# A fourth output buffer, an expert unit moved to another pair, and the last rows stored in two column halves

## The chip, the cores and the metric

The kernel runs on one core of one Trainium2 chip. The metric is the device time of one execution in microseconds, median of several runs. Before the change it is 336.73 us (three runs: 335.08, 336.73, 341.14). The profiled execution of it took 335.81 us, and its profile spans 334.1 us.

## The reference

Attention with a window and some global tokens over 8 batches of 8 heads, 576 tokens and 64 channels, then a feed-forward layer ("expert") with a squared ReLU over the 4608 tokens that come out:

```python
scores = scale * np.matmul(q, k.transpose(0, 1, 3, 2))        # per batch and head, 576 x 576
mask = np.abs(pos[:, None] - pos[None, :]) <= 32
mask = mask | is_global[:, None] | is_global[None, :]         # 8 global tokens
scores = np.where(mask, scores, -1e9)
attn = softmax(scores)
x = matmul(attn, v)  ->  (4608 tokens, 512)
h = x @ w_in                                                  # 512 -> 2048
r = np.maximum(h, 0.0)
out = (r * r) @ w_out                                         # 2048 -> 512, float32
```

## The kernel before

The attention of one batch is done in four pairs of heads. The expert layer works on chunks of 512 tokens, one chunk behind the attention, and is cut into units that are put between the steps of a pair, so that TensorE has work while ScalarE and VectorE (DVE) make the softmax. A chunk has 16 units of the first layer (`mm1`: four matmuls, a ReLU on ScalarE, a square on DVE) and 16 of the second (`mm2`: four row blocks of 128 tokens in four parts each; after the fourth part DVE copies the block from PSUM into an output buffer, and SyncE stores it).

```python
def expert_bank():                       # four PSUM banks in turn: three "mm", one "tr"
    banks["n"] += 1
    return pst("tr" if banks["n"] % 4 == 0 else "mm", [P, 512])

def mm1(c, u):
    ...
    for t in range(NDM):                 # 4
        nc.tensor.matmul(ph, w_in[:, t, u * P : (u + 1) * P], xT[:, t, ...], ...)   # L524
    rl = sbt("rl", [P, TC], FP16, bufs=3)
    nc.scalar.activation(out=rl, in_=ph, func=AF.Relu)                              # L529
    nc.vector.tensor_tensor(out=gts[c][:, u, :], in0=rl, in1=rl, op=ALU.mult)       # L530

def mm2(c, m, part):
    if part == 0:
        po_now[0] = expert_bank() if c else pst("mm", [P, 512])
    po = po_now[0]
    for f in range(part * 4, part * 4 + 4):
        nc.tensor.matmul(po, gts[c][:, f, m * P : (m + 1) * P], w_out[:, f, :], ...)  # L566
    if part == 3:
        ot = sbt("ot", [P, dm], FP32, bufs=3)
        nc.vector.tensor_copy(out=ot, in_=po)                                       # L572
        r0 = c * TC + m * P
        nc.sync.dma_start(out=out[r0 : r0 + P, :], in_=ot)                          # L574
```

One pair of heads, with `take(k)` issuing the next k units of the queue. `n` gives how many come before the outputs of the first half, between the two halves, and after the second half:

```python
def unit(i, n, nxt=None):
    scs = [scores(i, half, pair_tag[half], WIN2) for half in range(2)]     # matmuls, L621
    et = [weights(half, scs[half], WIN2) for half in range(2)]             # exp on ScalarE L630, mask on DVE L634
    take(n[0])
    ...
    for half in range(2):
        acc = outputs(i, half, et[half], pair_tag[half], WIN2, ...)        # matmuls, L663
        finish_outputs(i, half, acc, ...)     # ScalarE L686, L687: 1/sum; DVE L702 sums, L714 writes xT
        if half == 0:
            take(n[1])
    if i % NHP == NHP - 1:
        scatter(i // NHP)                     # DVE L733: the global tokens' rows into xT
    take(n[2])
```

The loop over the batches. In the first pair of a batch the copies of the next batch are put in: gathered and stored rows go through scratch memory, two transposing DMAs on SyncE bring the keys and queries, and five small copies on SyncE bring the values of the global tokens:

```python
for b in range(2, B):
    queue += units[b + 1]                     # one chunk: 32 units
    for hp in range(NHP):                     # 4 pairs
        unit(NHP * b + hp, ((2, 1, 4), (2, 1, 4), (2, 1, 5), (2, 1, 7))[hp])
        if hp == 0 and b + 1 < B:
            pool.tensor_copy(out=pin[0:1], in_=gsum[b][0:1, 0, 0, 0, 0:1])
            ...
            globals_to_scratch(b + 1)         # SyncE
            tokens_to_scratch(b + 1)          # GpSimd
            transposes(b + 1)                 # SyncE, L431
            vb[b + 1] = vb[(b + 1) % 2]
            values(b + 1)                     # GpSimd
            value_globals(b + 1)              # SyncE, L440
    take(99)
queue += units[B + 1] + units[B + 2]          # the last two chunks
take(999)
```

Of the kernel before, what the change touches and what calls it, by code (L numbers as in the profile page):

```python
# [8 lines left out]
FP32 = mybir.dt.float32  # L9
# [38 lines left out]
def kernel(  # L48
# [10 lines left out]
    nc = tc.nc  # L59
    B, H, S, D = q.shape  # L60
    NG = global_idx.shape[0]
    dm = H * D
    dff = moe_w_in.shape[1]
    P = 128
# [3 lines left out]
    NFF = dff // P  # L68
    NHP = H // 2
    TC = 512  # L70
    NCH = (B * S) // TC
# [6 lines left out]
    def sbt(name, shape, dtype, bufs=1, tag=None):  # L78
        return sb.tile(shape, dtype, name=name, tag=(tag or name), bufs=bufs)
# [5 lines left out]
    def pst(tag, shape, dtype=FP32):  # L85
        return ps.tile(shape, dtype, name=tag, tag=tag, bufs=bufs_of[tag])

    pool, dve, act = nc.gpsimd, nc.vector, nc.scalar
# [7 lines left out]
    w_out = sbt("w_out", [P, NFF, dm], FP16)  # L96
# [47 lines left out]
    for base, cu, cm in (  # L144
# [3 lines left out]
            out=ub[0], in_=ub[0], compare_op=ALU.is_ge, fill=0.0,  # L148
# [4 lines left out]
    for col, base, cm in ((slice(0, 2), -8, 1), (slice(1, 2), KN[-1] + 7, -1)):  # L153
        nc.gpsimd.affine_select(
            out=rows[:, col], in_=rows[:, col], compare_op=ALU.is_ge, fill=0.0,
# [3 lines left out]
        out=ub[1], in_=ub[0], compare_op=ALU.is_ge, fill=0.0,  # L159
# [9 lines left out]
        out=tok, in_=tok, compare_op=ALU.is_ge, fill=-1.0,  # L169
# [10 lines left out]
        out=identity, in_=identity, compare_op=ALU.not_equal, fill=1.0,  # L180
# [162 lines left out]
    def gather(c):  # L343
        for nm in "kqv":
            gst[(nm, c)] = sbt("gst" + nm, [P, D], FP16, bufs=2)
            pool.indirect_dma_start(
                out=gst[(nm, c)], out_offset=None,
                in_=src[nm].rearrange("b h s d -> (b h s) d"),
                in_offset=bass.IndirectOffsetOnAxis(ap=gidx[:, c : c + 1], axis=0),
            )  # L350
# [82 lines left out]
    def values(b):  # L433
        t = vb[b]
        for x in range(NT):
            fetch_values(b, x)
# [52 lines left out]
    def tr_k(i, op=None, tail=None, last=None, tag="mm"):  # L489
        op = op or dve.tensor_copy  # L490
        tk, gl = transposed("k", i, tag)
        kt = kts[i % NHP]
        op(
            out=kt[:, 0:4, 8:P].rearrange("p t (q j) -> p t q j", j=TJ),
            in_=tk[:, 0:80].rearrange("p (t q) j -> p t q j", t=4),
        )
        (tail or op)(
            out=kt[:, 4, 8 : 8 + KN[4]].rearrange("p (q j) -> p q j", j=TJ), in_=tk[:, 80:96]
        )
        (last or op)(out=kt[:, :, 0:NG], in_=gl.unsqueeze(1).to_broadcast((P, NT, NG)))  # L500

    def tr_q(i, op=None, tag="mm"):
        op = op or dve.tensor_copy
        tq, gl = transposed("q", i, tag)
        q4 = qts[i % NHP].rearrange("p (g x) -> p g x", x=GRP)
        op(
            out=q4[:, :, 0:GTOK].rearrange("p g (q j) -> p g q j", j=TJ),
            in_=tq.rearrange("p (g q) j -> p g q j", g=4),
        )
        op(out=q4[:, :, GTOK:GRP], in_=gl.unsqueeze(1).to_broadcast((P, 4, NG)))  # L510

    gts = {}
    banks = {"n": 0}

    def expert_bank():
        banks["n"] += 1
        return pst("tr" if banks["n"] % 4 == 0 else "mm", [P, 512])
# [40 lines left out]

    po_now = {}

    def mm2(c, m, part):
        if part == 0:
            po_now[0] = expert_bank() if c else pst("mm", [P, 512])
        po = po_now[0]
        for f in range(part * 4, part * 4 + 4):
            nc.tensor.matmul(  # L566
                po, gts[c][:, f, m * P : (m + 1) * P], w_out[:, f, :],
                start=(f == 0), stop=(f == NFF - 1),
            )
        if part == 3:  # L570
            ot = sbt("ot", [P, dm], FP32, bufs=3)
            nc.vector.tensor_copy(out=ot, in_=po)  # L572
            r0 = c * TC + m * P
            nc.sync.dma_start(out=out[r0 : r0 + P, :], in_=ot)  # L574

# [8 lines left out]
    queue = []  # L586

    def take(n):
        for _ in range(min(n, len(queue))):
            fn, a = queue.pop(0)  # L590
            fn(*a)
# [21 lines left out]
    def scores(i, half, tag, wins, sc=None):  # L613
        kt, qt = key_query(i)
        added = sc is not None
        if not added:
            sc = pst(tag, [P, 2, 512])
        for t, so, c0, w in wins[half]:
            for e in range(2):
                r = slice(64 * e, 64 * e + 64)  # L620
                nc.tensor.matmul(  # L621
                    sc[:, e, so : so + w], kt[r, t, :], qt[r, c0 : c0 + w],
                    start=not added, stop=True, skip_group_check=True,
                )
        return sc

    def weights(half, sc, wins, added=False):
        W = sum(x[3] for x in wins[half])
        et = sbt("et", [P, 2, SCW[0]], FP16, bufs=4)
        act.activation(  # L630
            out=et[:, :, 0:W], in_=sc[:, :, 0:W], func=AF.Exp, bias=0.0, scale=scale
        )
        if not added:
            dve.tensor_tensor(  # L634
                out=et[:, :, 0:W], in0=et[:, :, 0:W],
                in1=mask[:, MB[half] : MB[half] + W].unsqueeze(1).to_broadcast((P, 2, W)),
                op=ALU.mult,
            )
        return et
# [4 lines left out]
    def outputs(i, half, et, tag, wins, columns=False):  # L644
        b, hp = divmod(i, NHP)
        acc = pst(tag, [P, 2, 512])
        vt = vb[b]
        vtf = vt.rearrange("p t x d -> p t (x d)")
        nw = len(wins[half])
        for n, (t, so, c0, w) in enumerate(wins[half] if columns else ()):  # L650
            o = c0 - half * BANKC
            for x in range(2):
                for e in range(2):
                    nc.tensor.matmul(  # L654
                        acc[D * e : D * e + D, x, o : o + w],
                        one64 if x else vt[:, t, 4 * hp + 2 * e], et[:, e, so : so + w],
                        start=(n == 0), stop=(n == nw - 1), skip_group_check=True,
                    )
        for e in () if columns else range(2):
            for n, (t, so, c0, w) in enumerate(wins[half]):  # L660
                o = c0 - half * BANKC
                vo = D * (4 * hp + e)
                nc.tensor.matmul(  # L663
                    acc[:, e, o : o + w], vtf[:, t, vo : vo + P], et[:, e, so : so + w],
                    start=(n == 0), stop=(n == nw - 1), skip_group_check=True,
                )
        return acc
# [60 lines left out]
    def scatter(b, part=None, pairs=slice(0, NHP)):  # L728
        lo, hi = {
            None: (XOFF + b * S, XOFF + (b + 1) * S), 0: (0, HS + 1), 1: (XOFF + 255, XOFF + S),  # L730
        }[part]
        for g in range(NG):
            dve.tensor_copy(  # L733
                out=xT[:, pairs, lo:hi][:, :, ds(gvs[part][g], 1)],
                in_=gxs[b][:, pairs, g : g + 1],
            )
# [5 lines left out]
    def transposes0(hp):  # L742
# [11 lines left out]
        out=vb[0][0:NG, 0, 0 : 2 * H : 2], in_=idle[0:NG].rearrange("p (h d) -> p h d", d=D)  # L754
# [92 lines left out]
    def unit(i, n, nxt=None):  # L847
        scs = [scores(i, half, pair_tag[half], WIN2) for half in range(2)]
        et = [weights(half, scs[half], WIN2) for half in range(2)]
        take(n[0])  # L850
        if nxt:
            tr_k(nxt, tag="tr", tail=act.copy)
            tr_q(nxt, tag="mm", op=act.copy)
        for half in range(2):
            acc = outputs(i, half, et[half], pair_tag[half], WIN2, columns=i < 2 * NHP)
            finish_outputs(i, half, acc, columns=i < 2 * NHP)
# [3 lines that stand above are left out]
            scatter(i // NHP)  # L860
        take(n[2])
# [5 lines left out]
    for b in range(2, B):  # L867
        queue += units[b + 1]
        for hp in range(NHP):
            unit(NHP * b + hp, ((2, 1, 4), (2, 1, 4), (2, 1, 5), (2, 1, 7))[hp])  # L870
            if hp == 0 and b + 1 < B:
                pool.tensor_copy(out=pin[0:1], in_=gsum[b][0:1, 0, 0, 0, 0:1])  # L872
                if b == 2 or b % 2:
                    gather((b - 1) // 2)
                globals_to_scratch(b + 1)
                tokens_to_scratch(b + 1)
                transposes(b + 1)
                vb[b + 1] = vb[(b + 1) % 2]
                values(b + 1)
                value_globals(b + 1)  # L880
        take(99)
# [32 lines left out]
```

The softmax here doesn't subtract the row's maximum and nothing guards it: scores larger than these inputs give would overflow.

## Time and profile before

| what | value |
|---|---|
| device time, median of three runs | 336.73 us |
| profiled execution, span | 334.1 us |
| VectorE and ScalarE busy | 67% and 64% of the span |
| `L566` matmuls (second layer, "mm" banks) | 448, 103.9 us busy |
| `L524` matmuls (first layer, "mm" banks) | 384, 92.3 us busy |
| `L572` output copies | 36, 0.69 us each |
| stores of the output | 36, 256 KB each, on SyncE |

In what follows a line of a timeline has the start in us, the length, the engine, the line of the kernel, and the operation with its tiles; in brackets stand the idle time of the engine before it and what the profile names as its end. SPq lines are DMA issues on SyncE: their length is that of issuing, not of the transfer. Lines of stretches give for a window its length, then busy time (and number) of PE, PEld, DVE, ACT, POOL, then the granted TensorE clock, the busy share of the DMA engines and GB/s. A length of a matmul in the timeline is that of a pipelined instruction, so neighbours overlap.

### The profile page before, as it was taken

How to read it: one execution, taken by the hardware profiler on the slowest of the kernel's cores; microseconds unless marked ns; L12 is line 12 of the kernel's file. 1: busy time of each engine (PE TensorE's matmuls, PEld its weight loads, DVE VectorE, ACT ScalarE, POOL GpSimd, SP SyncE). 2: the span in 40 equal slices, each digit the busy share in tenths (PEclk: the TensorE clock that was granted, in tenths of full speed). 3: DMA queues.
4: the chain of work that ended last, by engine and by line, in shares of the span. 5: the costliest groups of instructions: out<-in, count | busy, mean ns of one | idle time of the engine just before them, and what ended most of it. 6: DMA issues, size and time to landing. Idle time of an engine off the chain costs nothing.

```text
span 334.1 us, 6749 instructions
## 1 busy us (share of the span) xinstructions
PE 317.7 (95%) x2377; PEld 163.6 (49%) x2377; DVE 224.1 (67%) x609; ACT 212.7 (64%) x425; POOL 106.7 (32%) x140
## 2 busy tenths in 40 slices
PE   7878899999999999899999999999999999999995
PEld 2557764444444544354545454445454554444442
DVE  7867955777768776687587866876878684323411
ACT  5777666669953995389539953896399626404600
POOL 8732477009900791078005930590000000000000
PEclk9999999999999999999999999999999999999999
DMA  7999999948996499899951999899710001011011
GB/s 203 189 204 207 203 160 139 172 138 61 143 143 169 32 139 134 178 100 134 121 169 33 123 140 175 114 130 141 128 63 3 31 33 63 0 65 63 1 65 63
DMA packets 148732, 38.20 MB, mean 114 GB/s; under 512 B 136802, under 2 KB 144090, under 8 KB 148698
## 3 DMA queue, kind: packets, MB, share of 16 engines
q0 software_dynamic: 104624, 17.37, 71.4%
q1 hardware_dynamic: 44072, 20.39, 31.6%
q8 instruction: 19, 0.31, 0.4%
q14 instruction: 15, 0.12, 0.1%
q10 hardware_dynamic: 2, 0.00, 0.0%
HBM read 37.36 MB, written 17.05 MB: 163 GB/s over the span
## 4 chain that ended last, share of the span: by engine, by line
PE 51%; ACT 22%; DVE 13%; DMA 6%; issue 5%; POOL 2%; DVEq 0%; ACTq 0%; POOLq 0%
PE mm L566 25%; PE mm L524 9%; ACT rl L529 8%; PE tr L566 7%; ACT et L630 7%; DMA vb<-in_v_dram 5%; ACT rec L686 4%; DVE xT L714 3%; PE tr L524 3%; DVE et L634 2%; ACT rec L687 2%; PE sc L663 2%; DVE xT L733 2%; PE acc L663 1%; DVE gt L530 1%
## 5 line engine op out<-in xcount | busy, mean ns | idle before, releaser
L566 PE MATMUL mm<-w_out,gt 128*128 128x512 f16 x448 | 103.9, 380 | 0.0
L524 PE MATMUL mm<-xT,w_in 128*128 128x512 f16 x384 | 92.3, 380 | 0.4 <-DVE xT L733 0.4
L566 PEld LDWEIGHTS <-gt 128*128 128x128 f16 x576 | 53.7, 98 | 60.3
L524 PEld LDWEIGHTS <-w_in 128*128 128x128 f16 x512 | 47.4, 98 | 53.4 <-issue 0.6
L529 ACT ACTIVATE rl<-mm 128x512 f16<-128x512 f32 x96 | 56.0, 598 | 27.2 <-PE mm L524 26.3
L530 DVE TENSOR_TENSOR gt<-rl 128x512 f16<-128x512 f16 x128 | 52.0, 424 | 16.9 <-ACT rl L529 14.7
L630 ACT ACTIVATE et<-sc 128x880 f16<-128x880 f32 (+1 forms) x32 | 29.0, 905 | 44.2 <-PE sc L621 44.2
L634 DVE TENSOR_TENSOR et<-et,mask 128x880 f16<-128x880 f16 x60 | 36.5, 615 | 24.6 <-ACT et L630 24.6
L114 POOL DMA_DIRECT2D vb<-in_v_dram x40 | 41.5, 1605 | 7.7 <-DMA w_out<-in_moe_w_out_dram 6.9
L524 PE MATMUL tr<-xT,w_in 128*128 128x512 f16 x128 | 32.9, 380 | 0.0
L714 DVE TENSOR_TENSOR xT<-sc,rec 64x288 f16<-64x288 f32 (+1 forms) x56 | 25.5, 455 | 8.8 <-ACT rec L687 8.4
L872 POOL COPY pin<-gsh 1x1 f32<-1x1 f32 x5 | 0.9, 177 | 92.1 <-DVE gsh L702 92.1
L572 DVE COPY ot<-mm 128x512 f32<-128x512 f32 x28 | 19.3, 689 | 16.3 <-PE mm L566 15.8
L687 ACT ACTIVATE rec<-rec 128x288 f32<-128x288 f32 x64 | 28.3, 443 | 2.0
L663 PEld LDWEIGHTS <-vb 128*128 128x128 f16 x288 | 21.3, 97 | 16.9 <-issue 6.9
L630 ACT ACTIVATE et<-acc 128x880 f16<-128x880 f32 (+1 forms) x32 | 29.1, 909 | 0.2 <-PE acc L621 0.2
L566 PE MATMUL tr<-w_out,gt 128*128 128x512 f16 x128 | 28.9, 379 | 0.0
L714 DVE TENSOR_TENSOR xT<-acc,rec 64x288 f16<-64x288 f32 (+1 forms) x56 | 25.5, 455 | 5.1 <-ACT rec L687 4.7
L686 ACT ACTIVATE rec<-sc 64x288 f32<-64x288 f32 (+1 forms) x56 | 22.8, 407 | 8.3 <-PE sc L663 6.1
L419 POOL DMA_DIRECT2D scr_k<-in_k_dram x30 | 26.6, 1093 | 2.6 <-DMA natq<-in_q_dram 1.5
L419 POOL DMA_DIRECT2D scr_q<-in_q_dram x24 | 24.9, 1599 | 0.9 <-DMA vb<-in_v_dram 0.9
L686 ACT ACTIVATE rec<-acc 64x288 f32<-64x288 f32 (+1 forms) x56 | 22.6, 404 | 1.9 <-PE acc L654 1.1
(132 smaller groups left out, 290.0 us busy)
## 6 DMA issues: line engine op xcount, KB each, us to landing
out_dram<-ot SPq DMA_DIRECT2D x36, 256.0 KB
vb<-in_v_dram POOLq DMA_DIRECT2D x29, 120.0 KB, 11.0
scr_q<-in_q_dram POOLq DMA_DIRECT2D x24, 144.0 KB, 5.5
scr_k<-in_k_dram POOLq DMA_DIRECT2D x24, 120.0 KB, 4.5
w_in<-in_moe_w_in_dram POOLq DMA_DIRECT2D x4, 512.0 KB, 12.9
w_out<-in_moe_w_out_dram POOLq DMA_DIRECT2D x4, 512.0 KB, 18.4
stk<-in_k_dram SPq DMA_DIRECT2D x4, 288.0 KB
stq<-in_q_dram SPq DMA_DIRECT2D x4, 288.0 KB
```

What stands on the lines that cost most here:

```text
L114: pool.dma_start(out=vb[b][NG - back : NG + KN[x], x, 2 * hs.start : 2 * hs.stop : 2], in_=v[b, hs, x * KT - back : x * KT + KN[x]].rearra ...
L419: pool.dma_start(out=scr[(nm, b % 2)][x * pitch + off : x * pitch + off + hi - lo].rearrange("s (h d) -> s h d", d=D), in_=src[nm][b, :, l ...
L524: nc.tensor.matmul(ph, w_in[:, t, u * P : (u + 1) * P], xT[:, t, XOFF + c * TC : XOFF + (c + 1) * TC], start=(t == 0), stop=(t == NDM - 1),)
L529: nc.scalar.activation(out=rl, in_=ph, func=AF.Relu)
L530: nc.vector.tensor_tensor(out=gts[c][:, u, :], in0=rl, in1=rl, op=ALU.mult)
L566: nc.tensor.matmul(po, gts[c][:, f, m * P : (m + 1) * P], w_out[:, f, :], start=(f == 0), stop=(f == NFF - 1),)
L630: act.activation(out=et[:, :, 0:W], in_=sc[:, :, 0:W], func=AF.Exp, bias=0.0, scale=scale)
L634: dve.tensor_tensor(out=et[:, :, 0:W], in0=et[:, :, 0:W], in1=mask[:, MB[half] : MB[half] + W].unsqueeze(1).to_broadcast((P, 2, W)), op=AL ...
L663: nc.tensor.matmul(acc[:, e, o : o + w], vtf[:, t, vo : vo + P], et[:, e, so : so + w], start=(n == 0), stop=(n == nw - 1), skip_group_che ...
L686: act.activation(out=rec[r], in_=av[rs, xs, :, 0:GTOK], func=AF.Ln)
L687: act.activation(out=rec, in_=rec, func=AF.Exp, scale=-1.0)
L714: dve.tensor_tensor(out=xT[r, hp, x0 : x0 + HS].rearrange("p (k x) -> p k x", k=2), in0=av[r, x, :, 0:GTOK], in1=rec[r], op=ALU.mult,)
```

## The change

Three things. The output tile gets a fourth buffer, so that the four row blocks of a chunk have one each. In each batch from the third on, the second pair of heads takes three expert units before its first outputs in place of two, and the fourth pair takes six units at its end in place of seven; the sum stays 32. And the last 128 rows of the output are no longer one product of 512 columns: they are made as two products of 256 columns, each with its own PSUM bank, copy and store, the first stored through SyncE's queue and the second through ScalarE's, so that the first half can leave while the second is computed.

```diff
+    def store(c, m, cols, po, queue):
+        w = cols.stop - cols.start
+        ot = sbt("ot", [P, dm], FP32, bufs=4)
+        dve.tensor_copy(out=ot[:, 0:w], in_=po[:, 0:w])
+        r0 = c * TC + m * P
+        queue.dma_start(out=out[r0 : r0 + P, cols], in_=ot[:, 0:w])
+
+    def last_rows_out(c, m):
+        for i, cols in enumerate((slice(0, dm // 2), slice(dm // 2, dm))):
+            po = expert_bank()
+            for f in range(NFF):
+                nc.tensor.matmul(
+                    po[:, 0 : dm // 2], gts[c][:, f, m * P : (m + 1) * P], w_out[:, f, cols],
+                    start=(f == 0), stop=(f == NFF - 1),
+                )
+            store(c, m, cols, po, nc.sync if i == 0 else act)
+
     def mm2(c, m, part):
+        if c == NCH - 1 and m == TC // P - 1:
+            if part == 0:
+                last_rows_out(c, m)
+            return
         if part == 0:
             po_now[0] = expert_bank() if c else pst("mm", [P, 512])
...
         if part == 3:
-            ot = sbt("ot", [P, dm], FP32, bufs=3)
-            nc.vector.tensor_copy(out=ot, in_=po)
-            r0 = c * TC + m * P
-            nc.sync.dma_start(out=out[r0 : r0 + P, :], in_=ot)
+            store(c, m, slice(0, dm), po, nc.sync)
...
-            unit(NHP * b + hp, ((2, 1, 4), (2, 1, 4), (2, 1, 5), (2, 1, 7))[hp])
+            unit(NHP * b + hp, ((2, 1, 4), (3, 1, 4), (2, 1, 5), (2, 1, 6))[hp])
```

## The prediction

> **What bounds the kernel now.** I read the busy shares first, then the share of the waits, then TensorE's timeline batch by batch, and last DVE's and SyncE's timelines around the widest gaps. The busy line of the page:
>
> ```profile
> PE 317.7 (95%) x2377; PEld 163.6 (49%) x2377; DVE 224.1 (67%) x609; ACT 212.7 (64%) x425; POOL 106.7 (32%) x140
> ```
>
> TensorE is the bound, but its 95% cannot be used for a sum: a 128x512 matmul is shown as 380 ns, while a unit of four starts 0.86 us after the one before. So I measure lost time as start to start. The queue serves 7, 7, 8 and 10 expert units in the four pairs of a batch. From the start of one pair's scores to the next the cleanest pairs take 7.40 us (7 units, e.g. 241.38 to 248.78), 8.26 (one unit more) and 9.99 (two more again). Against 7.40 / 7.40 / 8.26 / 9.99 the score starts on TensorE's timeline (69.83, 77.76, 85.34, 94.01, 104.86, 112.26, 119.84, 128.51, 138.50, 147.41, 154.81, 163.44, 173.43, 180.83, 188.41, 197.08, 207.07, 215.36, 222.76, 231.38, 241.38, 248.78, 256.36, 265.02, end 274.92) show these losses by pair: batch 2: 0.53, 0.18, 0.41, 0 (its last pair has 11 units, 10.85); batch 3: 0, 0.18, 0.41, 0; batch 4: 1.51, 0, 0.37, 0; batch 5: 0, 0.18, 0.41, 0; batch 6: 0.89, 0, 0.36, 0; batch 7: 0, 0.18, 0.40, 0. Sum 6.0 us of 205. That is all that an order of units or a buffer can give back in the batches; from 274.92 to 330 TensorE runs without a gap.
>
> TensorE's timeline in the second and third pair of batch 3 (start, length, then the work):
>
> ```profile
> 112.75 1.04 PE L524 MATMUL tr<-xT,w_in 128*128 128x512 f16 x4
> 113.62 1.03 PE L524 MATMUL mm<-xT,w_in 128*128 128x512 f16 x4
> 114.67 0.54 PE L663 MATMUL sc<-et,vb 128*128 128x160 f16 x6
> ...
> 121.20 1.03 PE L524 MATMUL tr<-xT,w_in 128*128 128x512 f16 x4
> 122.47 0.54 PE L663 MATMUL sc<-et,vb 128*128 128x160 f16 x6 [0.24 <-DVE et L634]
> ```
>
> The units start at 112.75 and 113.62, so the output matmuls could start at 114.48 and start at 114.67: 0.19 lost. In the third pair they could start at 122.06 and start at 122.47: 0.41 lost (the bracket shows less, as the modelled ends overlap). Both wait for the softmax weights: ScalarE, with 7 ReLUs a pair, runs without a pause here, from the exponential at 113.07 to that at 120.87, 7.80 us a pair against TensorE's 7.40.
>
> The widest gap, in the first pair of batch 4, is another. DVE's timeline, then SyncE's:
>
> ```profile
> 137.88 0.69 DVE L572 COPY ot<-mm 128x512 f32<-128x512 f32 x1
> 140.90 0.69 DVE L572 COPY ot<-tr 128x512 f32<-128x512 f32 x1 [2.33 <-PE mm L524]
> 141.50 1.13 DVE L634 TENSOR_TENSOR et<-et,mask 128x880 f16<-128x880 f16 x2
> ```
>
> ```profile
> 128.12 6.75 SPq L431 DMA_TRANSPOSE qb<-scr_q  x1
> 134.97 3.65 SPq L440 DMA_DIRECT2D vb<-gscr_v  x5
> 138.67 3.28 SPq L574 DMA_DIRECT2D out_dram<-ot  x4
> ```
>
> The fourth output copy of a chunk stands 2.33 us and holds the masking behind it on the same engine, and TensorE waits 1.28 us for that. The profile names a matmul, but the copy's own product was done at 138.5. The cause I read is the third output buffer: copy four needs the buffer of copy one, whose store sits on SyncE behind two transposes and five small copies and is issued only at 138.67; 2.23 us later the copy starts. The same at 206.52 and 208.84 (2.32 us), where the profile does name the store.
>
> **The Trainium skill.** "Perfetto Trace Analysis", Identifying Performance Opportunities, says that a bubble that repeats can mean too few buffers; here it does for batches 4 and 6, while the two small ones come from ScalarE's load. "DMA: Bandwidth & Descriptors", Anatomy of one DMA, gives a DMA a fixed cost of about 2.0 us besides its bytes; the trace shows 2.23 us from issue to release for 256 KB. The same page, Issuing engines are not separate DMA queues, says that a second queue saves only issue time; the trace agrees as far as it goes, with 0.33 us of issue. "VectorE: DVE Perf Modes", Why PSUM operands drop a tier, has fp32 reads of PSUM at the slowest rate, so time goes with columns: 0.69 us for 512 columns and 0.455 for 288 fit that.
>
> **Part 1, the fourth buffer.** Copy four then needs the buffer of a chunk ago, stored some 30 us before. It starts after copy three, as in batch 5 (172.82, then 173.54). That removes 1.51 and 0.89: 2.40 us. It uncovers the 0.18 of the second pair in these batches, which the stall had given ScalarE time to catch up with.
>
> **Part 2, the moved unit.** The instruction order shows one unit more before the outputs of the second pair, all later units one place earlier, and one fewer behind the last pair. Second pair: TensorE now arrives at 114.48 + 0.86 = 115.34, after the weights (114.67): gap 0.19 to 0. Third pair: ScalarE does one ReLU more before its exponential; in a row one costs 0.47 us (118.78 to 119.25), so outputs can start at 122.47 + 0.47 = 122.94. TensorE arrives at 122.06 - 0.19 + 0.86 = 122.73: gap 0.41 to 0.21. That is 0.39 us a batch.
>
> The price is at the batch's end. Count from the last pair's scores (231.38): DVE ends the scatter of the global tokens 9.34 us later (240.72). The next chunk's first unit starts at +10.48 (241.86); one unit less makes it +9.62, still 0.28 clear. Copies three and four follow at +9.38 and +10.10; from copy four's start to the output matmuls it takes 1.26 (140.90 to 142.16), so +11.36; TensorE arrives at 9.62 + 1.73 = +11.35. Both just fit. In batch 5 DVE had a pause of 0.29 in the scatter, so I charge 0.3 us in all for such cases. After batch 7 there are no scores in between: the next unit comes at +9.90 - 0.86 = +9.04 and must wait till about +9.40: 0.36 lost.
>
> Losses after: batch 2: 0.53 + 0.21; batches 3 to 6: 0.21 each; batch 7: 0.21 + 0.36; and 0.3: 2.45 in place of 6.0. Gain 3.55 us.
>
> **Part 3, the last rows.** The end of DVE's timeline, and the traffic of the last store:
>
> ```profile
> 330.37 0.69 DVE L572 COPY ot<-tr 128x512 f32<-128x512 f32 x1 [2.76 <-PE tr L566]
> ```
>
> ```profile
> 332.00:332.50 0.50, 0.00 (x0) 0.00 (x0) 0.00 (x0) 0.00 (x0) 0.00 (x0) 1.00 1.02 389
> 332.50:333.00 0.50, 0.00 (x0) 0.00 (x0) 0.00 (x0) 0.00 (x0) 0.00 (x0) 0.55 0.26 94
> ```
>
> Sixteen 512-column matmuls of 0.216 become 32 of 256 columns. This shape exists in the kernel: sixteen start 27.23 and the next work 29.08, 0.116 each. 32 x 0.116 = 3.70 in place of 3.45: +0.25. The last copy has 256 columns: by (0.69 - 0.455)/(512 - 288) = 1.05 ns a column, an estimate of 0.42: -0.27. The last store has 128 KB; each of 16 engines moves 8 packets of half the size, and the trace has medians of 85 ns for 2048 bytes and 59 for 1024: 8 x 26 = -0.2 to -0.35 with the start spread. The first half is stored meanwhile. Sum -0.3 us, with the ACT queue's start-up unknown.
>
> Total 3.55 + 0.3 = 3.9 us, 1.1%: from the median of 336.73, 332.8; in the span, 334.1 to about 330.3.
>
> **Rivals.** First: a wait that takes the place. The batch end is only 0.01 to 0.28 us clear; were DVE 0.3 later in each of five batches, 1.5 us come back: 334.3. For it: the pause of 0.29 and no slack; against: the other batches repeat 9.34 within 0.02. Second: the DMA chain. DMA engines are near full for long stretches, and the transposes end at 134.87 for scores at 138.50. If these data set the pace, shorter batches only turn into a wait for them: 335. Against: the chain is started by the first pair of the same batch, and TensorE comes only about 0.4 us earlier relative to that. Third: the stall is not the buffer; then part 1 gives nothing: 335.2. Against it: the two intervals of 2.23 and 2.32 after the issue, and no stall where the stores were issued early. Fourth: the second half finds the ACT queue slow, or small matmuls pay for weight loads (98 ns shown against 107 of streaming): the tail costs 0.5 and the time is 333.6. ScalarE as the new bound throughout is excluded: its ReLUs stay 7 or 8 before each exponential and it idles in the second half of each batch.
>
> **Range and chances.** The sum is a term of 2.4 that I trust, 1.2 made of tenths, and 0.3. The median before lies between 335.08 and 341.14, so a median of few runs may sit 1 us off: low 330.6, high 335.3. Faster by 2% would need 330.0, which even zero loss in the batches (6.0 + 0.3) misses: 0.04. Slower by 2% would need a new stall of over 1 us a batch: 0.01.
>
> **What would show it.** Right: no output copy held by a store; score starts 7.40 apart in all first and second pairs of batches 3 to 7; the third pair losing about 0.2; a wait for the scatter before the first unit after batch 7; last copy about 0.42. Wrong: first pairs of batches 3 to 7 over 7.5 (the batch end), a wait for a transpose or the value rows (the DMA chain), a second pair over 7.5 (ScalarE further behind), or more than 3 us from the last copy's end to the span's end.

## The result and the profile after

The changed kernel takes 332.11 us (median of six runs, 330.06 to 332.94); the kernel before 337.03. The ratio is 0.9857 with a 95% interval of 0.9817 to 0.9898: 4.9 us or 1.4% shorter, with 3.4 to 6.2 us inside the interval. The profiled execution took 331.81 us and spans 330.1, against 334.1 before: 4.0 us. The range on record, 330.6 to 335.3, holds the median; it lies 0.7 under the forecast.

The busy line of the changed kernel's page:

```profile
PE 316.8 (96%) x2393; PEld 165.4 (50%) x2393; DVE 223.9 (68%) x610; ACT 212.9 (64%) x425; POOL 107.6 (33%) x140
```

It says next to nothing, as before: the same work in a slightly shorter span. TensorE's timeline in the second and third pair of batch 3 says more (in the changed kernel scores are L639, outputs L681, second-layer units L587, the matmuls of the last rows L572, output copies L564, stores L566):

```profile
113.08 1.89 PE L524 MATMUL mm<-xT,w_in 128*128 128x512 f16 x8
114.81 0.54 PE L681 MATMUL sc<-et,vb 128*128 128x160 f16 x6
...
120.47 1.04 PE L524 MATMUL tr<-xT,w_in 128*128 128x512 f16 x4
121.34 1.03 PE L587 MATMUL mm<-w_out,gt 128*128 128x512 f16 x4
122.42 0.54 PE L681 MATMUL sc<-et,vb 128*128 128x160 f16 x6
```

Three units now stand before the outputs of the second pair, and these follow without a gap: 113.08 and two units of 0.86 give 114.81. In the third pair TensorE is ready at 122.20 and starts at 122.42: 0.22 lost, where 0.41 was lost before.

The end of batch 3 on DVE and SyncE:

```profile
135.71 3.17 SPq L566 DMA_DIRECT2D out_dram<-ot  x3
...
137.83 0.69 DVE L564 COPY ot<-mm 128x512 f32<-128x512 f32 x1
138.44 0.68 DVE L564 COPY ot<-tr 128x512 f32<-128x512 f32 x1
```

Copy four starts 0.61 us after copy three and no longer stands for a store. But there the first store was issued 2.73 us before it, so three buffers would have been enough. The end of batch 5 shows what the fourth does:

```profile
204.30 2.20 SPq L566 DMA_DIRECT2D out_dram<-ot  x4
...
205.15 0.68 DVE L564 COPY ot<-tr 128x512 f32<-128x512 f32 x1
```

Copy four starts 0.85 us after the first store's issue. In the five traces with three buffers it never starts less than 2.2 us after it.

The score starts, pair by pair as in the prediction, now give 7.93, 8.26, 8.48, 9.99 (batch 2); 7.40, 8.26, 8.48, 9.12 (batch 3); 7.40, 8.27, 8.47, 9.13 (4); 7.40, 8.26, 8.48, 9.66 (5); 7.41, 8.26, 8.48, 9.12 (6); 7.40, 8.27, 8.48, 9.40 (7). The clean values are 7.40, 8.26, 8.26 and 9.13. What is lost is 0.53 at the start of batch 2, 0.22 in each third pair, 0.37 after batch 7, and one thing that was not in the sum: 0.53 before batch 6.

```profile
204.65 0.37 PE L639 MATMUL sc<-qb,kb 64*128 64x160 f16 x6 [0.47 <-DMA qb<-scr_q]
...
271.47 2.75 PE L524 MATMUL mm<-xT,w_in 128*128 128x512 f16 x12 [0.20 <-DVE xT L751]
```

The first line waits for the transposed queries of batch 6, the second for the scatter after batch 7.

The last rows, in the kernel before and in the changed one:

```profile
326.72 3.62 PE L566 MATMUL tr<-w_out,gt 128*128 128x512 f16 x16
```

```profile
323.26 1.91 PE L572 MATMUL tr<-w_out,gt 128*128 128x256 f16 x16
325.01 1.91 PE L572 MATMUL mm<-w_out,gt 128*128 128x256 f16 x16
325.21 0.42 DVE L564 COPY ot<-tr 128x256 f32<-128x256 f32 x1 [1.06 <-PE tr L572]
326.96 0.42 DVE L564 COPY ot<-mm 128x256 f32<-128x256 f32 x1 [1.32 <-PE mm L572]
327.42 0.38 ACTq L566 DMA_DIRECT2D out_dram<-ot  x1
```

Sixteen 256-column matmuls take 325.01 - 323.26 = 1.75 us. From the first matmul of the last rows to the last copy's start: 3.65 before (326.72 to 330.37), 3.70 now. The copy: 0.69, now 0.42. From its end to the span's end: 3.04 before, 2.72 now. Together 7.4 and 6.8.

From the scores of batch 2 to the first unit after batch 7 it took 205.09 us and takes 201.81 (3.28 less); the stretch before it 69.83 and 69.66; the two last chunks up to the last rows 51.80 and 51.79; the end 0.54 less. That is the 4.0.

### The profile page after: what moved, and what is told of

Its sections match the earlier page's. It is cut to its first block, busy times and chain, and to the rows that moved or that the text cites. A ratio compares the mean times of both kernels' runs of the same rounds, so it can differ in the third digit from the quotient of the medians.

```text
span 330.1 us, 6785 instructions
## 1 busy us (share of the span) xinstructions
PE 316.8 (96%) x2393; PEld 165.4 (50%) x2393; DVE 223.9 (68%) x610; ACT 212.9 (64%) x425; POOL 107.6 (33%) x140
## 4 chain that ended last, share of the span: by engine, by line
PE 46%; ACT 23%; DVE 12%; DMA 9%; issue 6%; POOL 2%; SPq 0%; DVEq 0%; ACTq 0%; POOLq 0%
PE mm L587 22%; ACT rl L529 9%; PE mm L524 9%; ACT et L648 7%; PE tr L587 5%; DMA vb<-in_v_dram 5%; ACT rec L704 4%; DMA qb<-scr_q 4%; DVE xT L732 3%; PE tr L524 3%; ACT rec L705 2%; DVE et L652 2%; DVE xT L751 2%; PE sc L681 2%; DVE gt L530 2%
## 5 line engine op out<-in xcount | busy, mean ns | idle before, releaser
L587 PE MATMUL mm<-w_out,gt 128*128 128x512 f16 x448 | 104.9, 379 | 0.0
L524 PE MATMUL mm<-xT,w_in 128*128 128x512 f16 x384 | 90.8, 379 | 0.6 <-DVE xT L751 0.6
L587 PEld LDWEIGHTS <-gt 128*128 128x128 f16 x560 | 52.1, 98 | 58.1
L529 ACT ACTIVATE rl<-mm 128x512 f16<-128x512 f32 x96 | 55.1, 600 | 26.4 <-PE mm L524 25.8
L564 DVE COPY ot<-mm 128x512 f32<-128x512 f32 (+1 forms) x29 | 19.7, 679 | 17.5 <-PE mm L587 15.8
L681 PEld LDWEIGHTS <-vb 128*128 128x128 f16 x288 | 21.4, 98 | 12.6 <-issue 2.0
L587 PE MATMUL tr<-w_out,gt 128*128 128x512 f16 x112 | 25.3, 379 | 0.0
```

The source lines that it names most:

```text
L681: nc.tensor.matmul(acc[:, e, o : o + w], vtf[:, t, vo : vo + P], et[:, e, so : so + w], start=(n == 0), stop=(n == nw - 1), skip_group_che ...
```

## The experiments

Every kernel was timed in rounds beside the kernel before: it ran 6 to 22 times, the kernel before 22 to 45 times. The medians hold all runs; the ratios leave out those more than 1.5% above the fastest of their kernel. Because one execution differs from another by up to 2.9 us before the first scores of batch 2 (see the last section), traces are compared from there: "batches" is the time from these scores to the first unit after batch 7, 205.09 us for the kernel before and 201.81 for the changed one.

| kernel | time, us | ratio to before, 95% | span | batches |
|---|---|---|---|---|
| fourth buffer alone | 333.84 | 0.9921 [0.9892, 0.9950] | 330.8 | 203.04 |
| moved unit alone | 335.64 | 0.9974 [0.9950, 0.9997] | 334.0 | 204.88 |
| halves alone | 336.67 | 1.0002 [0.9972, 1.0031] | 333.9 | 204.69 |
| buffer and unit | 333.21 | 0.9897 [0.9856, 0.9938] | 331.1 | 201.92 |
| changed, halves on one queue | 332.83 | 0.9893 [0.9856, 0.9931] | 331.1 | 201.95 |
| before, no value-row copies | 334.42 | 0.9951 [0.9924, 0.9979] | 333.7 | 203.15 |
| changed, unit in third pair too | 331.68 | 0.9897 [0.9845, 0.9948] | 329.4 | 201.12 |
| changed, no value loads | 331.06 | 0.9843 [0.9806, 0.9880] | 329.7 | 201.26 |
| changed, early gathers | 330.97 | 0.9861 [0.9811, 0.9911] | 328.5 | 201.28 |
| third pair and early gathers | 330.62 | 0.9848 [0.9801, 0.9895] | 329.0 | 200.82 |
| all of these, and a bridge | 330.45 | 0.9861 [0.9813, 0.9909] | 328.3 | 201.23 |
| before, early gathers | 334.66 | 0.9958 [0.9935, 0.9982] | 331.8 | 204.03 |

**The fourth buffer alone.**

```diff
-            ot = sbt("ot", [P, dm], FP32, bufs=3)
+            ot = sbt("ot", [P, dm], FP32, bufs=4)
```

> The kernel before with the fourth output buffer alone. Theory (copy four waits for the late store of copy one): the losses of 1.51 and 0.89 us in the first pairs of batches 4 and 6 go, 0.18 comes back in their second pairs, third pairs still lose 0.41; span 334.1 - 2.4 + 0.4 = about 332.1. Rival (the copy waits for something else, as the profile names a matmul): both gaps stay, span 334.1 within 0.3.

The first pairs of batches 3 to 7 are all 7.40. The second pairs of batches 4 and 6, which had no loss before, lose 0.19 now, as expected; third pairs 0.40 to 0.41. The batches are 2.05 us shorter, where 2.40 - 0.36 = 2.04 was worked out. That they agree so well is partly luck: the first pair of batch 2 is 0.20 shorter in this execution, and 0.10 is lost before batch 6. DVE at the end of batch 5, and SyncE there:

```profile
203.92 0.69 DVE L572 COPY ot<-mm 128x512 f32<-128x512 f32 x1
204.53 0.68 DVE L572 COPY ot<-tr 128x512 f32<-128x512 f32 x1
205.30 1.90 SPq L574 DMA_DIRECT2D out_dram<-ot  x4
```

Copy four runs before even the first store of the chunk is issued, which with three buffers it cannot. So what the profile named in batch 4 of the kernel before, a matmul, was not what held the copy. In the runs the ratio gives 0.8%.

**The moved unit alone.**

```diff
-            unit(NHP * b + hp, ((2, 1, 4), (2, 1, 4), (2, 1, 5), (2, 1, 7))[hp])
+            unit(NHP * b + hp, ((2, 1, 4), (3, 1, 4), (2, 1, 5), (2, 1, 6))[hp])
```

> The kernel before with the moved unit alone, three buffers. Theory (coupled parts): TensorE comes 0.4 us earlier to the batch end, but copy four stays tied to the store, so the first-pair losses grow by what the second and third pair win, and batches whose store came just in time now stall too: span 0 to 1.0 us shorter, about 333.6. Rival (parts add up): 6 x 0.4 - 0.36 = 2.0 us shorter, 332.1.

The second pairs are at 8.26 and the third lose 0.13 to 0.23 with three buffers too, so that part needs no buffer. The batches are only 0.21 us shorter. The reason is not quite the expected one: the stalls behind the stores stay (first pairs of batches 4 and 6 at 8.46 and 8.00, so 1.06 and 0.60) but did not grow; 2.06 us were lost to another wait:

```profile
207.48 0.37 PE L621 MATMUL sc<-qb,kb 64*128 64x160 f16 x6 [1.99 <-DMA qb<-scr_q]
```

It is the wait for the transposed queries that the changed kernel shows with 0.47. Copy four again follows the store's issue, in batch 4 by 2.22 us:

```profile
137.63 3.28 SPq L574 DMA_DIRECT2D out_dram<-ot  x4
138.16 0.69 DVE L572 COPY ot<-mm 128x512 f32<-128x512 f32 x1
139.85 0.69 DVE L572 COPY ot<-tr 128x512 f32<-128x512 f32 x1 [1.00 <-DMA out_dram<-ot]
```

**The halves alone.** Of the diff only the functions `store` (with `bufs=3`) and `last_rows_out`.

> The kernel before with the last rows in two halves on two queues alone. From the two profiles the tail from the first matmul of the last rows to the end took 7.39 before and 6.84 after: 0.55 us shorter, span about 333.55, batches as before. Rival (the gain was in the batches alone): the same as before within 0.2.

In the trace the end takes 6.9 us (327.02 to 333.9) instead of 7.4, as expected. In the runs the ratio is 1.0002, and its interval of 0.3%, or 1 us, to either side is wider than the half microsecond that is sought: the runs neither show nor exclude it. The traces settle it: from the first matmul of the last rows to the end of the span it takes 7.39 to 7.46 us in the six kernels without the halves and 6.80 to 6.85 in the eight with them. This kernel has three buffers; TensorE loses 1.77 us in the first pair of batch 6 and nothing in that of batch 4, where DVE stands 0.68 for the store: how much the store costs changes between executions.

**Buffer and unit together.** The changed kernel without `last_rows_out`.

> The changed kernel without the halves: buffer and moved unit together. Theory (coupled): 4.0 - 0.55 = 3.4 us shorter than before, span about 330.7, more than the sum of buffer alone (2.0) and unit alone (0.5). Rival (parts add up): the sum of the other two kernels of this call.

The batches are 201.92, 3.17 less than before; the two alone gave 2.05 and 0.21, so in these traces 0.9 more together. But the 0.21 holds a wait of 2.06 that happened to fall there. By the runs, 0.9921 x 0.9974 = 0.9895 against 0.9897: they add up, within intervals of some 0.3 to 0.4%. That the parts need one another is not shown.

**Both halves on SyncE's queue.**

```diff
-            store(c, m, cols, po, nc.sync if i == 0 else act)
+            store(c, m, cols, po, nc.sync)
```

> The changed kernel with both halves of the last rows on SyncE's queue. Theory: the first half is issued over 1 us before the second is ready, so the second queue gives nothing: span 330.1 within 0.15. Rival (the second queue is what shortens the tail): 0.3 to 0.5 longer.

The end takes 6.8 us (324.30 to 331.1), the same as with two queues; the span is 1.0 longer, but 0.9 of that lies before batch 2 (70.55 against 69.66). The second queue gives nothing: the first half's copy ends at 326.67, more than a microsecond before the second half's at 328.41. What shortens the end is what lies behind the last matmul: the smaller copy (0.27) and the stretch of the smaller last store (0.32). In this execution 0.58 us went to a wait for the queries before batch 4 and 0.17, for which the profile names no DMA, were lost before batch 6: where that wait falls differs between executions of the same batches.

**Three buffers, stores earlier.** The kernel before, leaving out the copies of the global tokens' value rows for batches 3 to 7, so that these rows hold other values than the reference's.

```diff
-                value_globals(b + 1)
+                if b < 2:
+                    value_globals(b + 1)
```

> The kernel before, three buffers, leaving out the five small copies of the value rows of the global tokens for batches 3 to 7, which stand ahead of the stores on SyncE (3.65 us). Theory (the store of copy one is late only because of its place in SyncE's queue): stores are issued 3.6 us earlier, the first-pair gaps of batches 4 and 6 go with three buffers, span about 332.1 as with the fourth buffer. Rival: the gaps stay and the span is 334.1 within 0.3.

```profile
202.87 5.67 SPq L574 DMA_DIRECT2D out_dram<-ot  x4
206.88 0.69 DVE L572 COPY ot<-mm 128x512 f32<-128x512 f32 x1
207.49 0.68 DVE L572 COPY ot<-tr 128x512 f32<-128x512 f32 x1
```

The stores follow the transposes at once and copy four follows copy three, with three buffers. Counted from the start of batch 5, the transposes' issue ends at +29.2 and the first store is issued at +29.3; in the kernel before these are +29.3 and +33.1. The batches are 203.15, as with the fourth buffer (203.04). The span is 333.7 and not 332.1, since batch 2 began 1.45 us later than in the kernel before. In the runs the ratio gives 0.5%, less than the 0.8% of the buffer, with intervals that overlap. So the buffer was short because the store was late, and the store was late because of what stood ahead of it on SyncE.

**A unit more in the third pair.**

```diff
-((2, 1, 4), (3, 1, 4), (2, 1, 5), (2, 1, 6))[hp]
+(((2, 1, 4), (3, 1, 4), (3, 1, 4), (2, 1, 6)) if b < B - 1
+ else ((2, 1, 4), (2, 1, 4), (3, 1, 4), (2, 1, 7)))[hp]
```

> The changed kernel with three units also before the third pair's outputs and four behind them, and in the last batch (2,1,4), (2,1,4), (3,1,4), (2,1,7). Theory (what is left is ScalarE's lag in the third pair, 0.22 a batch, and the wait for the scatter after batch 7, 0.37): third pairs at 8.26 for eight units, span 330.1 - 1.3 = about 328.8. Rival (DMA chain): the keys and queries of the next batch come no earlier, first pairs wait for transposes in more batches, span 329.8 to 330.3.

Third pairs are at 8.26 to 8.27: the 0.22 is gone everywhere, and so is the wait after batch 7; the second pair of batch 7, again with two units ahead, loses 0.18. But the last pair of batch 5 takes 10.45 in place of the clean 9.13, and the batches win only 0.7 us in all, where the same sum without any more waiting for queries gives 1.5. The span, 329.4, lies between the two that were expected:

```profile
204.57 0.37 PE L639 MATMUL sc<-qb,kb 64*128 64x160 f16 x6 [1.25 <-DMA qb<-scr_q]
```

The scores of batch 6 start at 204.57, in the changed kernel at 204.65: in these two traces the queries came at the same time, and TensorE only stood in front of them longer.

**Without the value loads.** The changed kernel without GpSimd's loads of the values of batches 3 to 7, which so attend to old values.

```diff
-                values(b + 1)
+                if b < 2:
+                    values(b + 1)
```

> The changed kernel, leaving out GpSimd's loads of the values of batches 3 to 7 (attention of these batches uses old values). Theory (the 0.47 us wait for the transposed queries in batch 6 is the DMA engines' load): this wait goes, span about 329.5, and the times of its runs lie within 1 us. Rival (the transposes' own time or their start sets it): the wait stays, 330.1.

SyncE in batch 5, in the changed kernel and without the loads:

```profile
192.35 8.14 SPq L431 DMA_TRANSPOSE qb<-scr_q  x1
200.60 3.65 SPq L440 DMA_DIRECT2D vb<-gscr_v  x5
204.30 2.20 SPq L566 DMA_DIRECT2D out_dram<-ot  x4
```

```profile
192.38 2.33 SPq L431 DMA_TRANSPOSE qb<-scr_q  x1
194.82 4.08 SPq L440 DMA_DIRECT2D vb<-gscr_v  x5
198.94 7.39 SPq L566 DMA_DIRECT2D out_dram<-ot  x4
```

The transposes start at the same time, but issuing one takes 2.33 us in place of 8.14, and all behind it comes 5.4 us earlier. In all five batches the issue takes 2.2 to 3.0 us in place of 4.6 to 8.1. The wait before batch 6 is gone and the batches are 0.55 shorter. Its six runs lie between 330.48 and 331.96, 1.5 us apart, not within 1; the 22 of the kernel before, in the same rounds, 5.6 apart. The value loads, which run beside the transposes, are what makes queries and stores late here. By what part of the DMA path they do it was not tried.

**Gathers one batch earlier.**

```diff
-                if b == 2 or b % 2:
-                    gather((b - 1) // 2)
+                if b == 2:
+                    gather(0)
...
                 value_globals(b + 1)
+                if b in (2, 4):
+                    gather(b // 2)
```

> The changed kernel with the gathers of the global rows, which stand ahead of the token copies on GpSimd in batches 3 and 5, moved behind the value loads of batches 2 and 4. Theory (the wait for the transposed queries comes where a gather of over 3 us starts the DMA chain late): the wait before batch 6 (0.53 us with its pair) goes, span about 329.6. Rival (the value loads alone set it, as leaving them out took it away): the wait stays, 330.1.

SyncE in batch 5:

```profile
182.63 4.85 SPq L431 DMA_TRANSPOSE kb<-scr_k  x1
187.70 7.74 SPq L431 DMA_TRANSPOSE qb<-scr_q  x1
```

The batch begins at 169.74, so the queries' transpose starts at +17.96, against +21.50 in the changed kernel (192.35 - 170.85): 3.5 us earlier. From the end of the issue to the scores there are now 7.6 us, in the changed kernel 4.2. The last pair of batch 5 is at 9.13 and the batches are 201.28, 0.53 shorter. With the run before it this takes that wait away in two ways, each in one execution: start the chain earlier, or take load off it.

Another loss now shows. DVE pauses in the scatter of batch 5, as it does in all 14 traces (0.21 to 0.29 us), and TensorE no longer waits for the queries meanwhile, so the first pair of batch 6 takes 7.53, 0.13 over:

```profile
202.80 0.60 DVE L751 COPY xT<-gx 128x4 f16 x3 [0.21 <-DVE xT L751]
```

The two kernels that follow lose 0.14 there.

**Third pair and early gathers.** Both edits.

> Three units before the third pair's outputs too, and the early gathers. Theory: what the third pair won is no longer given back to the transposed queries (1.33 us of batch 5's last pair at 10.45 instead of 9.12): span 329.4 - 1.3 = 328.1. Rival: the wait stays, 329.4.

The wait before batch 6 is gone (9.13), the third pairs stay at 8.26; but batch 3 now waits for its queries, 0.87 us with its pair:

```profile
104.86 0.37 PE L639 MATMUL sc<-qb,kb 64*128 64x160 f16 x6 [0.80 <-DMA qb<-scr_q]
```

Batch 2 keeps its gather ahead of the tokens, and a second one runs in it now. Of the four kernels with early gathers, this one and the last one below wait there, the other two do not. Whether the second gather delays the queries was not tried. The span is 329.0, 0.4 shorter than without the early gathers where 1.3 was expected; that wait is the difference.

**All of these, and a bridge.** Also:

```diff
- b1=((2, 1, 2), (1, 1, 2), (1, 1, 2), (1, 1, 2))
+ b1=((2, 1, 2), (1, 1, 2), (1, 1, 2), (1, 1, 1))
...
- else ((2, 1, 4), (2, 1, 4), (3, 1, 4), (2, 1, 7))
+ else ((2, 1, 4), (3, 1, 4), (3, 1, 3), (2, 1, 7))
```

> As the one with early gathers and the third pair, and in the last batch (2,1,4), (3,1,4), (3,1,3), (2,1,7), and two old units instead of one left for the first pair of batch 2, which then bridge the wait for the scatter. Theory: 0.2 and 0.5 less than that kernel, span about 327.4, all first pairs at 7.40 but the one of batch 2. Rival: the bridge only moves the wait, 328.1.

In the last batch all pairs are clean (7.40, 8.27, 7.40). The bridge only moved the wait, as the rival had it: the first pair of batch 2 takes 8.54, as its second scores now stand for the rows of batch 1's last pair:

```profile
69.47 0.37 PE L639 MATMUL acc<-qb,kb 64*128 64x112 f16 x6 [0.71 <-DVE xT L732]
```

The batches hold one unit more here; 201.23 - 0.86 = 200.37. The span is 328.3, where 327.4 was expected and 328.1 by the rival. Its time, 330.45, is the lowest median, but its ratio 0.9861 [0.9813, 0.9909] is that of the changed kernel. It beats the kernel before; that it beats the changed kernel is seen in the batches of the traces (1.4 us) and not in the runs.

**The kernel before with early gathers.** Three buffers.

> The kernel before, three buffers, with the early gathers alone. Theory (the late stores, and so the stalls of copy four, come from the same late DMA chain, as they stand in the first pairs of batches 4 and 6, behind the gathers of 3 and 5): no stall, stores issued some 3 us earlier, span about 332.1, as with the fourth buffer. Rival (stores late for another reason): stalls stay, 334.1.

The stalls of batches 4 and 6 are gone: first pairs at 7.40. Stores come earlier, in batch 5 at 200.78, +28.99 from its start at 171.79 (206.52 - 173.43 = +33.09 before). So half of the theory holds. The rest does not: a stall of 2.16 us of DVE now stands at batch 3, where none was,

```profile
105.61 0.69 DVE L572 COPY ot<-tr 128x512 f32<-128x512 f32 x1 [2.16 <-DMA out_dram<-ot]
```

which costs TensorE 0.36 (a first pair of 7.76), and 0.73 us of the last pair of batch 2 go to a wait for the queries. The span of 331.8 looks like the theory's, but 1.2 of its gain lies before batch 2. The batches win 1.06 in place of 2, and the runs 0.4%, half of what the buffer gives. The buffer is the sturdier cure: in none of the nine traces with four buffers does a copy wait for a store.

## Why the prediction was right

**Part 1** held as worked out, the near-exact size (2.05 us for 2.04) partly by luck. There were too few output buffers: a fourth takes the stall of copy four away, an earlier store takes it away with three, and in every stalled case copy four starts 2.2 to 3.5 us after the first store's issue. What the prediction cites on too few buffers fits, though the stall did not repeat in every execution; what made them too few is the order on SyncE.

**Part 2** held to a few hundredths. Second pair: 0 lost, as forecast. Third pair: 0.22 lost for 0.21, as ScalarE's exponential comes at +16.50 from the batch's start in place of +16.01, 0.49 later for the 0.47 of one ReLU. After batch 7: 0.37 for 0.36. At the batch ends DVE just fitted, first pairs being 7.40 or 7.41.

**The reserve** of 0.3 us was set aside for DVE's lateness at the batch ends. In the changed kernel DVE cost nothing there, and the transposed queries cost 0.53 once. DVE's pause lay under that wait: where the queries came in time (the three changed kernels with early gathers) it cost 0.13 or 0.14, so the first rival held in one batch of five.

The queries are the second rival, and the step that failed is its dismissal. I set the transposes' end at 134.87 against the scores at 138.50, but 134.87 is the end of issuing. When the data landed these lines do not say. In the changed kernel the issue of batch 5 ended at 200.49 and TensorE was released at 204.65, 4.2 us later; in the other traces where the profile names this wait it was 4.2 to 6.4. It is no constant: in the kernel before the scores of batch 4 start 3.6 us after that end and wait for nothing. So the slack before batch 6 in the kernel before,

```profile
194.98 7.73 SPq L431 DMA_TRANSPOSE qb<-scr_q  x1
...
207.07 0.36 PE L621 MATMUL sc<-qb,kb 64*128 64x160 f16 x6
```

cannot be read from them. That it was small the runs show. Leaving out the kernels with early gathers and the one without value loads, all five with the moved unit lose time before batch 6 (0.53, 2.06, 0.66, 0.17 and 1.31 us), and the four without it 0.10 at most (for the 0.17 and the 0.10 the profile names no DMA). So the 0.4 us by which TensorE comes earlier was enough to meet the queries. The wait of 2.06 says that the queries also came later in some executions; why is open.

**Part 3**: the copy was 0.42 as estimated, and its end to the span's end 0.32 shorter for the 0.2 to 0.35 estimated. The term that was mis-sized is the matmuls: 0.109 us for 256 columns, and not the 0.116 taken from a stretch of sixteen that ended in another piece of work, so the two halves cost 0.05 more and not 0.25. Sum 0.54 for 0.3. The sentence on the second queue was right: it is worth nothing here.

**The total.** In the span 4.0 for 3.9, and that closeness is partly luck: the batches gave 0.3 less than the 3.55 forecast (3.28), the end gave 0.2 more, and 0.17 lies before batch 2, which is not the change's. The median fell by 4.9. The profiled execution of the kernel before, 335.81, lies 1.2 below the median of its runs, that of the changed kernel 0.3 below. The interval of 3.4 to 6.2 us holds the 4.0 of the traces as well, so the runs do not show that the change gives more. A late store may cost more in other executions than in the profiled one; these were not traced, so that stays open.

## What to carry to other kernels

Look up what stands ahead of a store in its queue before counting buffers: a buffer is held from its copy until its store lands, and here the store waited behind two transposes and five small copies, so three buffers were short though a store takes only 2.2 us from its issue to the release of its buffer. When an engine wins tenths at a place where several chains meet, read the margin of each other chain up to its landing, not to the end of its issue; here the next wait was that one, and in the third-pair run it took 0.8 of 1.5 us.

## What the runs showed of the hardware that was not expected

- Issuing the DMA transpose of the queries took 8.14 us while the value loads ran and 2.33 without them; where TensorE waited for the queries, it was released 4.2 to 6.4 us after the issue had ended, and elsewhere it started 3.6 us after it without a wait. Neither is seen in the transpose's own line.
- The scores of batch 2 began between 68.4 and 71.3 us in the 14 traces, with nearly the same instructions before them. A difference of under 3 us between the spans of two single executions means little; counted from there, the clean pairs agree within 0.02 us (7.40 and 8.26).
